# Buffer of the spectrum parts for a last transform: token pair outermost instead of channel half

## The chip, the cores and the metric

One core of a Trainium2 chip. The time is the device time of one execution in microseconds (us), as a median over several executions. A profile is one further execution, recorded by the hardware; its span runs from the first to the last instruction and is about 2 us shorter than the time. Of the engines, TensorE multiplies matrices, VectorE adds, ScalarE copies and applies functions, and the sync engine (SP) starts transfers (DMA); ScalarE starts some too. A trace also records the clock that TensorE was granted, 1.00 being full speed; it is called "half clock" at 0.50.

## The reference

Two branches on the same normalised input, added up, 2048 tokens of 512 channels:

```python
xn = _layernorm(x, axis=-1)
return x + _A_ref(xn, ...) + _B_ref(xn, ...)
# _A_ref: long convolution over the tokens by FFT of length 4096, plus u * Dskip
#   Yf = rfft(u, padded) * rfft(K, padded);  y = irfft(Yf)[:L]
# _B_ref: gated MLP of width 1792
#   h = sigmoid(x @ w_gate) * (x @ w_up);  return h @ w_down
```

The convolution is done as a transform in several stages of matmuls. What matters here is its last stage: it multiplies the "spectrum parts" by a constant matrix, and its result is added to that of the MLP.

## The kernel before: the parts that matter

The spectrum parts come from DRAM scratch (`v_scr`, one for each channel half p) into one SBUF buffer, 16 loads of 256 KB. Index p is the channel half (256 channels), t the token pair, r the token of the pair, j a half of the contraction.

```python
vall = at(0, [NP, 8, 2, 2, DW])        # NP = 2, DW = 256: [p, t, j, r, channel], 32 KB per partition
vps = [[vall[:, p, t] for t in range(8)] for p in range(NP)]
for t in range(8):
    for p in range(NP):
        ...   # dma("SP" if p == 0 or t % 2 == 0 else "ACT", vps[p][t], ...)   256 KB

def s2_mm(t, r, o, start, ps=(0, 1)):  # the last transform of one token pair
    kw = dict(stop=True, skip_group_check=True)
    i = 2 * t + r
    w = slice(DW * ps[0], DW * ps[-1] + DW)
    for j in range(2):
        T.matmul(o[:, w], s2[:, j, :], vall[:, ps[0]:ps[-1] + 1, t, j, r, :], start=start and j == 0, **kw)
    if i >= 12:
        T.matmul(o[:, w], sr[:, i - 12, :], rr[:, w], start=False, **kw)
```

One matmul thus reads 256 elements of each half. The program runs a fixed order of work (a long list in the source). Which instruction waits for which is not written by hand: the compiler layer derives it from the pieces of the buffers that each instruction reads and writes. Towards the end TensorE's order is: down projection of 14 matmuls; t=5; down projection; first row of t=6; t=0; second row of t=6; t=3; t=1; down projection; first row of t=7; t=4; t=2; down projection; the two channel halves of the last row of t=7. Line L994 is the `T.matmul` over `vall`, L996 the correction with `sr`, L1074 the down projection, L1009 and L1091 VectorE's additions, L973 the copy into `rr`, L417 every DMA issue.

## Time and profile before

| | before |
|---|---|
| time, median of the first three runs | 249.63 us (249.52 to 250.48) |
| span of the profiled run | 247.2 us |
| TensorE busy | 227.4 us, 92% |
| VectorE, ScalarE busy | 187.6 us, 181.6 us |
| idle of TensorE ahead of the last transform | 1.60 + 0.25 + 5.39 us |

A share of 92% suggests that little is to be had. Read by slices, TensorE is full until 217 us and has holes after that. The lines that show it are in the prediction. One more stretch matters later, the 3.4 us just ahead of the fall of the clock (length, busy time and count by engine, granted clock, DMA share, GB/s):

```profile
223.20:226.60 3.40, 1.37 (x7) 0.40 (x5) 1.82 (x2) 0.00 (x0) 0.00 (x0) 1.00 0.44 123
226.60:233.44 6.84, 3.48 (x9) 1.34 (x10) 0.98 (x2) 0.00 (x0) 0.00 (x0) 0.50 0.30 94
```

TensorE was busy for 1.37 of the 3.40 us, and then had half clock for 6.84 us.

### The profile page before, as it was taken

To read this page: it belongs to the slowest core of one execution; us is meant where nothing else is said; L and a number is where in the kernel's file an instruction comes from. 1 tells how busy PE (TensorE), PEld (TensorE's weight loads), DVE (VectorE), ACT (ScalarE), POOL (GpSimd) and SP (SyncE) were. 2 spreads that over 40 slices of the span, in tenths; PEclk is the share of its full clock that TensorE was granted. 3 is DMA by queue.
4 is the path that set the end of the run, shared out by engine and by line. 5 is a ranking of instruction groups with operands and counts; after the bars stand their busy time and mean duration, and the time that the engine had idled before them with its cause. 6 is when DMAs were issued, how large, how long until landed. Compare 5 with 4: busy or idle time off the path is not lost.

```text
span 247.2 us, 5353 instructions
## 1 busy us (share of the span) xinstructions
PE 227.4 (92%) x2045; PEld 114.2 (46%) x2074; DVE 187.6 (76%) x397; ACT 181.6 (73%) x294; POOL 18.4 (7%) x42
## 2 busy tenths in 40 slices
PE   7979999999999999999999999989999998972793
PEld 3545444444344643656556454366543553421341
DVE  3999899999999999999999999922344175512342
ACT  5989999999999986799988999764577785000000
POOL 1205200020000101000103100000000300000000
PEclk9999999999999999999999999999999999998699
DMA  6999775203496873756684676747776977935033
GB/s 153 213 376 334 246 264 127 87 11 74 137 231 216 164 191 97 165 172 191 140 223 109 208 199 163 174 133 231 198 195 217 187 228 196 266 89 180 16 140 115
DMA packets 50859, 43.60 MB, mean 176 GB/s; under 512 B 12561, under 2 KB 44050, under 8 KB 50834
## 3 DMA queue, kind: packets, MB, share of 16 engines
q1 hardware_dynamic: 48738, 40.58, 58.1%
q0 software_dynamic: 864, 1.57, 4.1%
q10 hardware_dynamic: 1232, 1.11, 1.5%
q8 instruction: 16, 0.26, 0.5%
q14 instruction: 9, 0.07, 0.1%
HBM read 24.64 MB, written 12.06 MB: 148 GB/s over the span
## 4 chain that ended last, share of the span: by engine, by line
PE 45%; ACT 21%; DMA 17%; SPq 7%; issue 5%; DVE 4%; ACTq 0%; DVEq 0%
PE bank L1074 12%; PE bank L1026 9%; DMA big<-v_scr 6%; PE bank L1041 5%; SPq L417 5%; PE pair L913 5%; PE pair L820 4%; ACT hT_sb L1035 4%; DMA big<-z_scr 4%; ACT big L697 3%; ACT big L666 3%; DMA wd_sb<-in_B_w_down_dram 3%; DMA wg_sb<-in_B_w_gate_dram 3%; PE pair L994 3%; ACT big L672 2%
## 5 line engine op out<-in xcount | busy, mean ns | idle before, releaser
L1026 PE MATMUL bank<-xnT,wg_sb 128*128 128x512 bf16 (+1 forms) x224 | 54.4, 368 | 2.6 <-DMA wg_sb<-in_B_w_gate_dram 1.0
L1041 PE MATMUL bank<-xnT,wu_sb 128*128 128x512 bf16 x215 | 53.5, 379 | 0.8 <-issue 0.3
L1074 PE MATMUL bank<-wd_sb,hT_sb 128*128 128x512 bf16 x217 | 50.5, 379 | 0.9 <-ACT glu_sb L1104 0.3
L1035 ACT ACTIVATE hT_sb<-bank 128x512 bf16<-128x512 f32 x56 | 33.2, 612 | 4.4 <-PE bank L1026 4.3
L1026 PEld LDWEIGHTS <-wg_sb 128*128 128x128 bf16 x236 | 21.6, 98 | 26.7 <-issue 5.3
L1074 PEld LDWEIGHTS <-hT_sb 128*128 128x128 bf16 x224 | 21.4, 98 | 26.2 <-issue 1.6
L1041 PEld LDWEIGHTS <-wu_sb 128*128 128x128 bf16 x224 | 21.2, 98 | 25.3 <-issue 2.0
L1056 DVE TENSOR_TENSOR hT_sb<-hT_sb,bank 128x512 bf16<-128x512 bf16 x36 | 23.9, 682 | 9.6 <-PE bank L1041 6.2
L919 DVE TENSOR_TENSOR big<-big 128x2048 bf16<-128x2048 bf16 x16 | 19.4, 1217 | 15.4 <-ACT big L915 8.0
L731 DVE TENSOR_TENSOR big<-big 128x1024 bf16<-128x1024 bf16 (+4 forms) x40 | 25.8, 644 | 0.6 <-ACT big L772 0.3
L732 DVE TENSOR_TENSOR big<-big 128x1024 bf16<-128x1024 bf16 (+4 forms) x40 | 25.7, 643 | 0.0
L913 PE MATMUL pair<-big 128*128 128x256 bf16 x160 | 19.8, 272 | 0.4 <-DVE big L855 0.3
L900 ACT ACTIVATE big<-pair 128x1024 bf16<-128x1024 f32 x16 | 16.3, 1025 | 4.3 <-PE pair L895 4.1
L915 ACT ACTIVATE big<-pair 128x1024 bf16<-128x1024 f32 x16 | 16.5, 1035 | 3.8 <-PE pair L913 3.1
L940 ACT ACTIVATE big<-pair 128x1024 bf16<-128x1024 f32 x16 | 16.3, 1033 | 2.8 <-PE pair L936 1.2
L913 PEld LDWEIGHTS <-big 128*128 128x128 bf16 x160 | 15.6, 98 | 5.5 <-issue 1.2
L697 ACT ACTIVATE big<-pair 128x1024 bf16<-128x1024 f32 x16 | 16.9, 1056 | 0.2 <-DMA z_scr<-big 0.2
L736 DVE TENSOR_TENSOR big<-big 128x512 bf16<-128x512 bf16 (+4 forms) x40 | 16.8, 420 | 0.2
L737 DVE TENSOR_TENSOR big<-big 128x512 bf16<-128x512 bf16 (+4 forms) x40 | 16.8, 419 | 0.0
L788 ACT ACTIVATE sq_sb<-big 128x256 bf16<-128x256 bf16 (+2 forms) x20 | 13.0, 655 | 2.6 <-DVE big L737 2.0
L666 ACT ACTIVATE big<-big 128x512 bf16<-128x512 f32 x24 | 14.0, 644 | 0.0
L772 ACT ACTIVATE big<-big 128x256 bf16<-128x256 bf16 x32 | 13.1, 454 | 1.1 <-PE pair L820 1.1
(106 smaller groups left out, 276.1 us busy)
## 6 DMA issues: line engine op xcount, KB each, us to landing
big<-c_E SPq DMA_DIRECT2D x16, 320.0 KB, 4.2
z_scr<-big SPq DMA_DIRECT2D x16, 256.0 KB, 2.6
big<-z_scr SPq DMA_DIRECT2D x16, 256.0 KB, 4.3
big<-big SPq DMA_DIRECT2D x64, 64.0 KB, 3.1
v_scr<-big SPq DMA_DIRECT2D x16, 256.0 KB, 3.0
big<-v_scr SPq DMA_DIRECT2D x12, 256.0 KB, 4.6
big<-in_A_u_dram SPq DMA_DIRECT2D x4, 512.0 KB, 5.5
wu_sb<-in_B_w_up_dram SPq DMA_DIRECT2D x2, 896.0 KB, 8.7
```

What stands on the lines that cost most here:

```text
L666: S.activation(out=W[p][:, k], in_=cur[:, :, DW * p:DW * p + DW], func=ACT.Identity)
L697: ev = pl.add("ACT", 0.90, lambda sl=sl, zs=zs: S.activation(out=zs().rearrange("p j d -> p (j d)"), in_=two(sl), func=ACT.Identity), [fx_ ...
L731: V.tensor_tensor(out=wide(outp), in0=wide(lo), in1=mre, op=ALU.mult)
L732: V.tensor_tensor(out=wide(tb()), in0=wide(lo), in1=mim, op=ALU.mult)
L736: V.tensor_tensor(out=outp[:, :, :, 0, :], in0=outp[:, :, :, 0, :], in1=tb()[:, :, :, 1, :], op=opr)
L913: T.matmul(two(sk)[:, o:o + DW], es()[:, g, kt, :], kT[p][:, kt, :], start=kt in (0, NKT - 1), stop=kt >= NKT - 2)
L919: V.tensor_tensor(out=pp().rearrange("p q h m -> p (q h) m"), in0=xx().rearrange("p q h m -> p (q h) m"), in1=kb()[:, 0:2 * DW].unsqueeze( ...
L1026: T.matmul(bank(sl)[:, c0:c1], w[:, kt, k * 128:(k + 1) * 128], xnT[:, grp, kt, c0:c1], start=(kt == 0), stop=(kt == KT - 1))
L1035: S.activation(out=hT_sb[:, hs.idx, k % 2, :], in_=bank(sl), func=ACT.Sigmoid)
L1041: T.matmul(bank(sl), wu_sb[:, kt, k * 128:(k + 1) * 128], xnT[:, grp, kt, :], start=(kt == 0), stop=(kt == KT - 1))
L1056: V.tensor_tensor(out=h(), in0=h(), in1=us_sb[:, us.idx, :] if on else bank(sl), op=ALU.mult)
L1074: T.matmul(bank(po), hT_sb[:, hts[k // 2].idx, k % 2, jj * 128:(jj + 1) * 128], wd_sb[:, k, :], start=(k == 0), stop=k == FT - 1, **kw)
```

## The change

Its intent is that all that belongs to one token pair lies together, so that a read of one pair spans no other pair's parts.

```diff
-    vall = at(0, [NP, 8, 2, 2, DW])
-    vps = [[vall[:, p, t] for t in range(8)] for p in range(NP)]
+    vall = at(0, [8, NP, 2, 2, DW])
+    vps = [[vall[:, t, p] for t in range(8)] for p in range(NP)]
@@ s2_mm
-            T.matmul(o[:, w], s2[:, j, :], vall[:, ps[0]:ps[-1] + 1, t, j, r, :], ...)
+            T.matmul(o[:, w], s2[:, j, :], vall[:, t, ps[0]:ps[-1] + 1, j, r, :], ...)
```

More of the change, by code (lines that the diff above doesn't have):

```diff
@@ L993, in s2_mm @@
         for j in range(2):
-            T.matmul(o[:, w], s2[:, j, :], vall[:, ps[0]:ps[-1] + 1, t, j, r, :], start=start and j == 0, **kw)
+            T.matmul(o[:, w], s2[:, j, :], vall[:, t, ps[0]:ps[-1] + 1, j, r, :], start=start and j == 0, **kw)
         if i >= 12:
```

## The prediction

> **What bounds the kernel now.** I read the page's slices first, then the chain that ended last, then the last 40 us engine by engine, because the change touches one buffer that is only read at the end. The slices:
>
> ```profile
> PE   7979999999999999999999999989999998972793
> ...
> PEclk9999999999999999999999999999999999998699
> ```
>
> Up to slice 35 TensorE is the bound, busy nine tenths or more at full clock. From slice 36 (222 us) that breaks: 7, 2, 7, and the granted clock falls in the same place. So 25 us at the end are limited by something else. The chain over 208 us to the end (start, length, what) says what:
>
> ```profile
> 211.22 7.31 DMA big<-v_scr
> 218.53 0.05 issue
> 218.58 1.05 PE pair L994 x4
> 219.63 0.02 issue
> 219.65 3.19 DMA big<-v_scr
> 222.84 0.05 issue
> 222.89 0.61 PE bank L994 x2
> ...
> 225.92 0.34 SPq L417
> 226.26 0.05 issue
> 226.32 3.61 DMA big<-v_scr
> 229.92 0.04 issue
> 229.96 1.01 PE bank L994 x2
> 230.98 0.43 PE bank L996
> 231.40 2.79 PE pair L994 x8
> ```
>
> Three times the last transform (L994) waits for a load of spectrum parts into `vall`, until 218.58, 222.89 and 229.96. TensorE's timeline gives the idle times as 1.60, 0.25 and 5.39 us. Why are those loads so late? ScalarE's queue and the waits of the sync engine's queue answer:
>
> ```profile
> 210.59 9.58 ACTq L417 DMA_DIRECT2D big<-v_scr  x3
> 220.22 0.59 ACT L973 ACTIVATE big<-pair 8x512 bf16<-8x512 f32 x1 [9.51 <-PE pair L994]
> ...
> SPq L417 <- PE bank L994: 10.5, 1, 10.5
> ```
>
> Queue instructions that only start loads of `v_scr` wait for matmuls of L994 on ScalarE (9.5 us, the rr copy stuck behind) and on the sync engine (10.5 us, once). A load into a slot that no matmul has read yet should wait for no matmul.
>
> The cost of the long wait is more than its length (busy time and count by engine, granted clock, DMA share, GB/s):
>
> ```profile
> 224.60:229.96 5.36, 0.00 (x0) 0.10 (x1) 1.82 (x2) 0.00 (x0) 0.00 (x0) 0.69 0.65 196
> 229.96:233.40 3.44, 3.44 (x9) 1.20 (x9) 0.94 (x2) 0.00 (x0) 0.00 (x0) 0.50 0.00 0
> ```
>
> After the hole the matmuls run at half clock until about 233.4.
>
> **What the compiled program says.** I listed the semaphore waits of the kernel before as compiled (a list of instructions, no time in it). Write p for the channel half and t for the token pair. A matmul of pair t reads `vall[:, 0:2, t, j, r, :]`: 256 elements of p=0 and 256 of p=1. With p outermost these lie 16 KB apart, and the dependence tracker treats everything between as read. So the first one (t=5) waits not only for its own parts (0,5) and (1,5), but for (0,6), (1,0), (1,1), every other load ahead of it in program order that lies in that interval. The other way round, load (1,3) waits for the matmuls of t=5, and load (1,4) for those of t=6 (as if it overwrote them), and the matmuls of the second row of t=6 wait for (1,4) and (1,2). None of these is a true dependence.
>
> **What the Trainium skill says.** "Perfetto Trace Analysis", section "Identifying Dependency Chains", says to look at the instruction's own text for the semaphores it waits on, and that extra conditions can sit in an event instruction ahead of it; that is how I found the list above, and the trace has such event instructions on L994. "TensorE: Matmul & The Clock Gate", section "What's actually happening", gives half clock after an idle window of about 3.4 us and full clock after a busy one. The trace agrees: the mean of 0.69 over 224.60 to 229.96 means that 62% of it, 3.3 us, was at 0.50, so the half clock began at 226.6 and lasted to about 233.4, two such windows. "DMA: Bandwidth & Descriptors", section "Queues, rings and completion order", says each DMA engine takes turns between the queues' rings and takes a ring in order; so a load that is added behind another on the same queue should not slow that one much. The trace of before cannot show that. No page bears on how waits are derived from access patterns.
>
> **The change part by part.** It removes and adds no instruction: the same 16 loads of 256 KB, the same matmuls, the same order on each queue. Each load still writes 2 KB in a row per partition, each matmul still moves 2 x 256 elements. What changes is the address: the four reads of pair t now lie inside a block of 4 KB that belongs to t alone. All false waits go, in both directions. The half (0,t) moves up to at most 28 KB; the tables that lived there are last read by L820, whose last group ends at 163.8, and the first load of `vall` is issued at 165.18, so no new wait comes in.
>
> Now the tail again, in TensorE's unchanged order, with full-clock durations from the same trace. The first matmul needs (1,5), whose semaphore in the trace is complete at 217.00, not (1,1), complete at 218.53. The down projection before it ends at 216.98 (218.58 less 1.60). So:
> - t=5: 217.05 + 1.05 = 218.10.
> - Down projection of 14 matmuls, 3.02 (as 239.59 to 242.61): 221.12.
> - t=6 first row with its correction matmul, 0.65 (as 237.22 to 237.87): 221.77.
> - t=0, 0.88 (as 223.71 to 224.59): 222.65. t=6 second row: 223.30.
> - t=3 and t=1, 1.73 (as 237.87 to 239.60): 225.03.
> - Down projection: 228.05. t=7 first row: 228.70. t=4 and t=2: 230.43. Down projection: 233.45.
>
> In the kernel before the last of these ends at 242.62. Difference 9.17 us, which is: 1.53 (first wait), 0.24 and 0.17 (second wait, and the slow start after it), 5.37 (third wait), 0.79 and 1.07 (matmuls of t=6, t=3, t=1 at half clock). What follows, the last two half rows, two additions and the stores, is 4.58 us in both. All of the 9.17 lies on the path that sets the end.
>
> Is everything else there in time? Loads: (1,3) is issued about 212.7, just behind (1,1); (1,4) about 213.5, when its semaphore lane is free (212.97); (1,7) after the rr copy, about 215. All loads before them had landed at 218.5. At the 320 to 380 GB/s that the DMA view shows from 213 to 216 these three, 768 KB, take some 2.4 us more: by 221. (1,3) is needed at 223.3, (1,7) at 228.05, (1,4) at 228.7. Load (1,2) keeps its place behind the store of t=0, which waits for VectorE: t=0 ready at 222.65, addition 1.23 us, store issued 224.0, load issued 224.4, landed 3.6 later, 228.0; needed by t=2 at 229.6. VectorE: additions of t=0, t=6 (two of 0.68), t=3 end about 226.5, t=1 about 227.8 (it waits for a store to free its buffer); TensorE needs their PSUM at 228.7 and 229.6. It fits, with 1 to 3 us of slack each.
>
> **Rivals.**
> 1. The waits are real or come from somewhere else, so nothing moves: 249.6. For it: the three waits are all named as DMA, and the profile names only the last releaser. Against: the queue waits on L994 for 10.5 us, and the list of waits.
> 2. The loads are hidden no better, because the traffic is the limit. The DMA share is 0.92 from 209 to 217. If loads issued earlier slow (1,5), the first wait comes back: at worst 1.5 us, time 242. If load (1,2) behind the stores turns out late, t=2 waits 1 or 2 us, and the last down projection with it: 242 too. A short hole like that would not halve the clock.
> 3. The hole at 224.6 goes but the clock stays low, say by a hole of over 2 us elsewhere: 1.9 us of the gain lost, 242.3.
> 4. A layout cost: operand halves 2 KB apart instead of 16 KB. L994 matmuls at full clock have the same 379 ns as L1074's with contiguous operands, so I see no penalty to gain or lose: 0.
>
> **Range and chances.** 249.63 - 9.2 = 240.4 us. Rivals 2 and 3 push up by at most about 2; downwards I see 1 us (first matmuls after no wait start faster, 0.88 for 1.05; fewer event instructions; stores earlier). Range 239.3 to 242.3. Faster by over 2% means below 244.6; only rival 1 or two of the others together get there: 0.96, 0.03, 0.01.
>
> **What would show it.** Span near 238. In the chain no load of `v_scr` after the first t=5; no wait of the queues on L994; the idle time of L994 below 0.5 us in all but the last half row (0.51 for VectorE, which stays); granted clock 1.00 from 217 on; rr copy at 214 in place of 220; everything before 209 unchanged. It would be wrong if the sync queue still waits for L994, if (1,5) lands after 218, or if the chain shows stores or VectorE between the groups of L994.

## The result

240.56 us median (240.04 to 241.47, 4 runs) against 249.81 us of the kernel before (4 runs). The ratio is 0.963, 95% interval 0.959 to 0.967. Ratios here are the mean time of one kernel's fast runs over that of the other's of the same rounds, so not quite the ratio of the medians quoted. The instructions on each engine are the same ones in the same order. The slices of the changed kernel (PE is the busy share of TensorE in tenths, PEclk its granted clock in tenths):

```profile
PE   7989999999999999999999999999999989799993
...
PEclk9999999999999999999999999999999999999999
```

The dips at the end and the fall of the clock are gone. The chain that ended last, from 211 us to 228 us:

```profile
211.74 5.70 DMA big<-v_scr
217.44 0.02 issue
217.46 1.02 PE pair L994 x4
218.48 3.02 PE bank L1074 x14
221.50 0.43 PE bank L994 x2
221.93 0.21 PE bank L996
222.15 0.86 PE pair L994 x4
223.01 0.43 PE bank L994 x2
223.44 0.22 PE bank L996
223.66 1.75 PE pair L994 x8
225.41 3.02 PE bank L1074 x14
```

After t=5 no load stands in the chain, to its end: one TensorE group follows on the other, and the last two half rows alternate with VectorE's additions. (The chain dates the load from 211.74, the issue of (1,1). By the semaphores the last one that t=5 waits for is (1,5), issued at 211.10 and complete at 217.41; (1,1) was complete at 219.19, after t=5 had started.) The queues, in the same two places as before, ScalarE's timeline and then the sync queue's waits (engine and line, waited for: total, times, longest):

```profile
211.10 2.27 ACTq L417 DMA_DIRECT2D big<-v_scr  x3
214.41 0.59 ACT L973 ACTIVATE big<-pair 8x512 bf16<-8x512 f32 x1 [3.23 <-PE pair L971]
...
SPq L417 <- DVE big L1009: 13.9, 6, 4.5
SPq L417 <- ACT big L940: 3.8, 2, 2.4
SPq L417 <- DMA big<-in_A_u_dram: 2.2, 1, 2.2
```

ScalarE's three loads go out in 2.27 us instead of 9.58, and the copy into `rr` runs at 214.4 instead of 220.2. The sync queue's wait of 10.5 us for L994 is gone; what it waits for now (L1009) are stores that wait for VectorE's results.

### The profile page after: what moved, and what is told of

Same layout as the page of the kernel before. It is cut to its first block, busy times and chain, and to the rows that moved or that the text cites. A ratio compares the mean times of both kernels' runs of the same rounds, so it can differ in the third digit from the quotient of the medians.

```text
span 238.5 us, 5382 instructions
## 1 busy us (share of the span) xinstructions
PE 227.5 (95%) x2074; PEld 113.8 (48%) x2074; DVE 187.5 (79%) x397; ACT 181.6 (76%) x294; POOL 18.4 (8%) x42
## 4 chain that ended last, share of the span: by engine, by line
PE 42%; ACT 24%; DMA 14%; DVE 7%; SPq 6%; issue 5%; ACTq 0%; DVEq 0%
PE bank L1074 15%; DMA big<-big 9%; PE bank L1026 7%; ACT hT_sb L1035 5%; SPq L417 4%; PE pair L913 4%; PE bank L1041 4%; ACT big L666 3%; PE pair L820 3%; ACT big L697 3%; DMA wg_sb<-in_B_w_gate_dram 3%; ACT big L672 3%; DVE big L919 2%; DMA big<-v_scr 2%; ACT big L558 2%
## 5 line engine op out<-in xcount | busy, mean ns | idle before, releaser
L1026 PE MATMUL bank<-xnT,wg_sb 128*128 128x512 bf16 (+1 forms) x236 | 55.4, 369 | 1.6 <-DMA wg_sb<-in_B_w_gate_dram 0.9
L1041 PE MATMUL bank<-xnT,wu_sb 128*128 128x512 bf16 x224 | 54.5, 380 | 0.1
L919 DVE TENSOR_TENSOR big<-big 128x2048 bf16<-128x2048 bf16 x16 | 19.4, 1219 | 16.1 <-DMA big<-big 6.8
L936 PE MATMUL pair<-big 64*64 64x512 bf16 (+1 forms) x256 | 13.0, 327 | 1.4 <-DVE big L919 1.4
```

The lines of the kernel that those rows point to most:

```text
L919: V.tensor_tensor(out=pp().rearrange("p q h m -> p (q h) m"), in0=xx().rearrange("p q h m -> p (q h) m"), in1=kb()[:, 0:2 * DW].unsqueeze( ...
L1026: T.matmul(bank(sl)[:, c0:c1], w[:, kt, k * 128:(k + 1) * 128], xnT[:, grp, kt, c0:c1], start=(kt == 0), stop=(kt == KT - 1))
L1041: T.matmul(bank(sl), wu_sb[:, kt, k * 128:(k + 1) * 128], xnT[:, grp, kt, :], start=(kt == 0), stop=(kt == KT - 1))
```

## The experiments

Two theories stood against each other. The first: the gain is that of waits that were never needed, since a strided read counts as a read of all that lies between its pieces. The second: the addresses themselves matter, where the loads write or how far apart the two pieces lie. Each experiment but the last two starts from the kernel before. Line numbers shift by a few in some; L996, L997, L998 and L999 are then the `vall` matmul or its correction.

**1. Layout of before, reads split.**

```diff
+        for qs in [(q,) for q in ps]:
+            w = slice(DW * qs[0], DW * qs[-1] + DW)
             for j in range(2):
-                T.matmul(..., vall[:, ps[0]:ps[-1] + 1, t, j, r, :], ...)
+                T.matmul(..., vall[:, qs[0]:qs[-1] + 1, t, j, r, :], ...)
```

> The layout of before (halves 16 KB apart), but each matmul of the last transform reads one half only, so no read spans another pair's parts; twice as many matmuls, half as wide. Theory (false waits from the span of a read): no load waits for a matmul, no hole before the last half row, clock 1.00 to the end, time as after: 240.5, at most 0.5 more for the extra weight loads. Rival (the addresses themselves matter, where the loads write or how far apart the operand's halves lie): the loads go where they went before, so most of the hole stays, 247 to 250.

Measured: 240.64 us, ratio 0.963 (0.960 to 0.966), the same as the change. TensorE's timeline:

```profile
217.32 1.20 PE L997 MATMUL pair<-big 128*128 128x256 bf16 x8
218.36 3.18 PE L1077 MATMUL bank<-wd_sb,hT_sb 128*128 128x512 bf16 x14
221.38 0.38 PE L997 MATMUL bank<-big 128*128 128x256 bf16 x2
```

No idle time stands in brackets. Every load writes where it wrote before, and the whole gain is there. That rules out the addresses of the loads.

**2 and 3. Halves 4 KB apart, two groupings.** Pairs share a block by twos; in the second kernel which two is chosen so that each false wait is for a load that lands early.

```diff
-    vall = at(0, [NP, 8, 2, 2, DW])
-    vps = [[vall[:, p, t] for t in range(8)] for p in range(NP)]
+    vall = at(0, [NP * 8, 2, 2, DW])
+    place = {t: n for n, t in enumerate(range(8))}                   # experiment 2
+    place = {t: n for n, t in enumerate((0, 1, 4, 2, 3, 7, 5, 6))}   # experiment 3
+    unit = lambda p, t: place[t] // 2 * 4 + place[t] % 2 + 2 * p
+    vps = [[vall[:, unit(p, t)] for t in range(8)] for p in range(NP)]
@@ s2_mm
-            ... vall[:, ps[0]:ps[-1] + 1, t, j, r, :] ...
+            ... vall[:, unit(ps[0], t):unit(ps[-1], t) + 1:2, j, r, :] ...
```

> Halves 4 KB apart, so that pairs 0 and 1, 2 and 3, 4 and 5, 6 and 7 share a block and have false waits only within it. Theory: the first and the second wait are gone, but the matmuls of t=3 now wait for load (1,2), which sits on the sync queue behind the store of t=0: one hole of about 4.5 us before t=3, from 223.6 to 228.1, with or without a time at half clock after it: 245 to 246.5. Rival (distance matters): close to after, 240.5 to 241.5.

> Halves 4 KB apart as in the run before, but blocks shared by pairs 0 and 1, 4 and 2, 3 and 7, 5 and 6: there are still false waits, each on a load that has landed long before. Theory: a false wait costs only if its releaser is late, so as after: 240.5 within 0.7, no hole. Rival (distance, or any false wait costs): same as the run with the natural grouping.

Measured: 248.24 us (ratio 0.993, 0.988 to 0.997) for the natural grouping, 240.66 us (0.965, 0.959 to 0.971) for the other. The regrouped kernel has no idle time ahead of t=3 and t=1:

```profile
225.85 1.91 PE L996 MATMUL pair<-big 128*128 128x512 bf16 x8
```

The same distance gives nearly nothing or the whole gain, by grouping alone. So distance is not the cause, and neither is the bare number of foreign parts that a read spans (one in both kernels). What counts is whether the load falsely waited for comes late. In the first of the two kernels that load is (1,2), which has its place on the sync queue behind the store of t=0. Its chain:

```profile
222.79 1.24 DVE big L1011
224.03 0.02 issue
224.05 0.34 SPq L417
224.39 0.05 issue
224.44 3.43 DMA big<-v_scr
227.87 0.05 issue
227.92 3.60 PE pair L996 x8
```

The addition of t=0, its store, the load, then t=3: a loop through VectorE and two DMA issues that t=3 does not need. The hole came as expected, until 227.9. The time did not: 1.7 us over the range. The windows say why:

```profile
224.00:229.00 5.00, 1.08 (x3) 0.44 (x4) 1.22 (x3) 0.00 (x0) 0.00 (x0) 0.79 0.36 105
229.00:232.00 3.00, 3.00 (x8) 1.06 (x7) 1.67 (x2) 0.00 (x0) 0.00 (x0) 0.50 0.02 7
232.00:236.00 4.00, 3.95 (x15) 1.62 (x15) 0.78 (x1) 0.00 (x0) 0.00 (x0) 0.78 0.52 192
```

By the trace the clock was at half from 226.92 to 233.74, and matmuls ran in 5.8 us of that. The eight matmuls of t=3 and t=1 took 3.60 us instead of 1.73, the down projection after them 4.18 instead of 3.02: 3 us of loss. In the kernel before the matmuls came late in the half-clock stretch and lost less. So a shorter hole (4.57 us) cost more after it than a longer one.

**4 and 5. Fill the hole.** Idle matmuls into an unused bank of PSUM (the memory that takes TensorE's results), in the kernel before (23, ahead of the second row of t=6) and in experiment 2 (19, ahead of t=3).

```diff
         i = 2 * t + r
+        if i == 13:                      # i == 6 and 19 in the other
+            for _ in range(23):
+                T.matmul(banks[2][:], hT_sb[:, 0, 0, 0:128], wd_sb[:, 0, :], start=True, stop=True)
```

> The kernel before with 23 idle matmuls of 512 columns (their result is not used) put on TensorE just ahead of the second row of t=6, where the hole of 5.4 us is. The false waits stay. Theory: the hole is filled and stays as long, but the clock no longer halves: the terms for half clock, 0.79 and 1.07 us, are saved, 247.8 to 248.2, granted clock 1.00 from 224 on. Rival: the half clock is not caused by the hole (a fixed time after the start, or the power drawn): unchanged 249.8 with 0.50 in the same place.

> The run with halves 4 KB apart came out at 248.2 instead of 245 to 246.5; its profile has the hole that was expected (4.57 us before t=3) but 3 us of half clock cost rather than at most 1: the half clock lasted 6.8 us, nearly all of it over matmuls. Here 19 idle matmuls fill that hole. If that reading is right: hole and false wait stay, clock 1.00 to the end, 248.2 - 3.0 = 245.2, within 0.7. If something else held it up: 247 or more.

Measured: 247.53 us (ratio 0.992, 0.989 to 0.995), by medians 1.84 us less than before, where the prediction's two terms for half clock add up to 1.86. And 244.81 us (ratio 0.981, 0.977 to 0.986) for the filled one of experiment 2. That is 3.4 us less than without by medians, 2.8 by the ratios (the two did not run in the same rounds); 3.0 was expected. Useless work made both kernels faster, since it kept the clock up. The window of the hole, filled, in the kernel before:

```profile
224.60:229.96 5.36, 4.88 (x24) 2.22 (x23) 1.76 (x2) 0.00 (x0) 0.00 (x0) 1.00 0.65 196
229.96:233.40 3.44, 3.44 (x18) 1.55 (x17) 2.71 (x3) 0.00 (x0) 0.00 (x0) 1.00 0.00 0
```

The granted clock is 1.00 in both stretches, and in the second 18 matmuls fit where the kernel before had 9.

**6. Only t=5 split.** The edit of experiment 1, for t == 5 alone.

> The kernel before with the reads of the first pair used, t=5, split into halves, the others left as they were. Theory, term by term: the first wait (1.53) and the second (0.24 and 0.17) go, the hole before the second row of t=6 stays, since load (1,4) still waits for the first row of t=6 and load (1,2) sits behind the stores; then the clock halves. The terms of the working give 249.4 - 1.9 = 247.5; [...]247 to 248.5. A hole of about 5.3 us that ends near 228. Rival (the three waits overlap, so the first two are absorbed by the third): 249.4.

Measured: 248.04 us (ratio 0.994, 0.989 to 0.998).

```profile
217.40 0.81 PE L997 MATMUL pair<-big 128*128 128x256 bf16 x6 [0.22 <-DMA big<-v_scr]
...
221.07 0.59 PE L997 MATMUL bank<-big 128*128 128x512 bf16 x2
...
228.25 1.01 PE L997 MATMUL bank<-big 128*128 128x512 bf16 x2 [5.51 <-DMA big<-v_scr]
```

The first wait is down to 0.22 us, the second is gone, and the hole ends 1.7 us earlier than before. It is as long as before: what comes earlier ahead of it moves it whole. Of the 1.7 about 1.1 went to the clock: half clock lasted from 227.10 to 233.93, and the work from the hole's end through the next down projection took 8.35 us instead of 7.26.

**7. Only t=6 split**, the pair that the profile names at the long wait.

> The kernel before with only the reads of t=6 split, the pair in front of which TensorE stood idle for 5.4 us. Theory: the hole only moves on by one group, since the matmuls of t=3 span load (1,2) as well: about 4.7 us of idle before t=3, ending near 229.5, then half clock. The first wait of 1.5 stays. 248 to 249.5, a gain of 1.4 at most. Rival (what the profile names, a wait of t=6, is the cause by itself): the 5.4 us and the half clock go, 242 to 243.

Measured: 248.91 us over its three fast runs (ratio 0.997, 0.991 to 1.002; the fourth run, 252.0 us, was slow). No gain can be told. The chain:

```profile
226.05 0.34 SPq L417
226.40 0.05 issue
226.45 3.59 DMA big<-v_scr
230.04 0.04 issue
230.08 3.60 PE pair L997 x8
```

The second row of t=6 no longer waits, and t=3, next in line, waits for the same load until 230.08. The waiter that a profile names is the first in line, not all of the cause.

**8. Loads first, layout of before.** The four loads that follow the first matmul in program order are moved ahead of it.

```diff
+        early = (623, 625, 631, 621)          # loads (1,3), (1,4), (1,7), (1,2)
+        seq = [n for n in ORDER if n not in early]
+        at_ = seq.index(619) + 1              # behind load (1,1)
+        seq[at_:at_] = early
-        for n in ORDER or range(len(self.ops)):
+        for n in seq:
```

> The kernel before with the four late loads moved ahead of the first matmul of the last transform in program order, layout as before. No load can wait for a matmul any more (that direction is gone), but the first matmul, t=5, spans all loads from (0,5) to (1,5), now among them (1,2), (1,3), (1,4). Theory: one hole of 4 to 4.5 us in front of t=5, until about 221.5, then none; 244.5 without a time at half clock, up to 247.5 with one, as in the run with 4 KB. Rival (only loads that wait for matmuls cost): 240.5 to 241.

Measured: 246.71 us (ratio 0.989, 0.985 to 0.994).

```profile
222.15 1.87 PE L998 MATMUL pair<-big 128*128 128x512 bf16 x4 [4.54 <-DMA big<-v_scr]
223.81 3.91 PE L1078 MATMUL bank<-wd_sb,hT_sb 128*128 128x512 bf16 x14
...
217.00:221.60 4.60, 0.61 (x3) 0.19 (x2) 0.00 (x0) 0.00 (x0) 0.00 (x0) 1.00 0.84 275
221.60:225.00 3.40, 2.85 (x7) 0.99 (x7) 0.95 (x1) 0.00 (x0) 0.00 (x0) 0.54 0.02 5
```

With one direction of false waits gone (loads for matmuls), the other (the first matmul for all loads in its span) makes a hole of 4.54 us, and half clock follows. Both directions count. Reordering alone does not replace the layout.

**9. Can more be had? The last row in two halves**, on the changed kernel, beside that kernel again.

```diff
-    for k in range(FT):                       # last down projection, 512 columns in one bank
-        T.matmul(bank(po), hT..., wd_sb[:, k, :], ...)
+    # 256 columns into one PSUM bank, last transform of that half; then 256 into another bank
+    down(0); s2_mm(7, 1, bank(po), False, (0,))
+    down(256)                                 # VectorE adds and SP stores the first half meanwhile
```

> The changed kernel, with the last down projection done in two halves of 256 columns, each in a PSUM bank of its own, and the first half finished (last transform, addition, store) while the second is being multiplied. In the changed kernel the second half row waits 0.52 us for VectorE's addition to the first, since both lie in one bank. 28 matmuls at about 0.109 us each take 3.05 us instead of 3.02. The second half row then ends at once: about 0.6 us less than the changed kernel beside it, so about 239.9 against 240.5. If the last addition isn't on the path, or weight loads are not hidden with 256 columns: no gain or a loss of up to 1 us.

> The changed kernel again, beside the run with the last halves on the same chip: 240.5, ratio to before 0.963 as measured first. Only for that comparison.

Measured in five rounds: 239.86 us (ratio to before 0.961, 0.958 to 0.965) and 240.15 us (0.963, 0.959 to 0.966) for the changed kernel beside it. In the profile the idea works: TensorE's last groups are

```profile
230.57 1.69 PE L1074 MATMUL bank<-wd_sb,hT_sb 128*128 128x256 bf16 x14
232.09 0.38 PE L994 MATMUL bank<-big 128*128 128x256 bf16 x2
232.31 0.27 PE L996 MATMUL bank<-big 128*128 128x256 bf16 x1
232.42 1.69 PE L1074 MATMUL bank<-wd_sb,hT_sb 128*128 128x256 bf16 x14
233.95 0.38 PE L994 MATMUL bank<-big 128*128 128x256 bf16 x2
```

with no idle time between the halves, where the changed kernel waits 0.52 us. But the two intervals overlap nearly whole. A gain of 0.3 us is possible and not shown.

## Why the prediction was right

- *False waits as the cause.* Shown from two sides: experiment 1 removes them without the layout, experiment 3 keeps the strided reads and false waits but makes them harmless, and both come out with the change. Rival 1 (nothing moves) has fallen. Rival 3 did not come true in the profiled run: the granted clock is 1.00 until 237.50, after the last matmul. Rival 4 has fallen too: `vall` matmuls at full clock have a median of 379 ns before and after.
- *The sum.* Predicted from the first matmul of t=5 to the end of the last down projection: 217.05 to 233.45, 16.40 us. Measured: 217.46 to 233.82, 16.36 us. Counted from the start of t=5, the groups hit their place to 0.1 us. The span was 238.5 instead of 238.0 mainly because t=5 came 0.4 us later, and so had the last projection ahead of it (214.24 against 213.78), in a stage that the change does not touch: there TensorE waited 1.43 instead of 0.73 us for VectorE (L919, until 206.4). The other 0.1 us lies behind the last projection. So "everything before 209 unchanged" held only to half a microsecond. Other profiles shift too: t=5 starts at 217.15 in that of experiment 2 and at 219.81 in that of experiment 3, after the half clock at 199 us named below; that run (242.83 us) is the slowest of its four.
- *The first wait, 1.53.* The term holds as a cause: the first matmul no longer waits for (1,1). In experiment 6 it shrank to 0.22. It ends where predicted, at the landing of (1,5), which by now lands as the down projection ends.
- *Half clock, 0.79 + 1.07.* Experiment 4 confirms the term and its size roughly. That 1.84 by medians meets the 1.86 so closely is luck: the interval of its ratio means 1.3 to 2.9 us. In its trace the groups from the end of the hole to the next down projection take 2.53 instead of 4.24 us, so 1.71, and the hole ended 0.28 us earlier besides. It is a term of this kernel, not a constant: in experiment 2 the same kind of stretch cost 3 us. The expectations of experiment 2 took over the small size, and there missed by 1.7 us.
- *What the prediction had wrong about the clock.* It says that the trace agrees with half clock after an idle window of about 3.4 us. The half clock did last two such times (6.83 us), but it began 2.0 us after the last matmul had ended (224.57, 226.61), so the 3.4 us before it were not idle. Under rivals 2 and 3 it says that a hole of 1 or 2 us would not halve the clock and one of over 2 us might. In the profiled run of experiment 3 a wait of 2.10 us for a load (until 198.55) was followed by half clock from 199.37 to 202.78, so that limit has hardly any room. Nothing of the 9.17 us rests on either sentence; the upper end of the range did.
- *Rival 2, the traffic.* Three more loads were issued while (1,5) was in flight. It took 6.3 us from issue to completion (211.10 to 217.41), before 6.4 (210.59 to 217.00). Two of the three went behind it on its own queue, ScalarE's. The Trainium skill, "DMA: Bandwidth & Descriptors", section "Queues, rings and completion order", says a ring is taken in order, from which the prediction concluded that what is queued behind should not delay it much; this trace agrees. The third went on the sync engine's queue, behind two loads that were there before as well. Load (1,2) was issued at 224.75 (predicted 224.4) and nothing waited for it.
- *The terms cannot be removed one at a time.* The sum counted 5.37 us for the long wait. Experiment 7 removed its named waiter and gained nothing that can be told. The prediction used the terms only for the change as a whole, where they do add up.

## What to carry to other kernels

Where a framework derives waits from access patterns, lay a shared buffer out so that what one instruction reads in a stride is one block that nothing else writes; splitting the read does the same. Look in the profile for a load that waits for a matmul which never used its slot, and list the waits of all later readers before you believe that removing the named one helps. Count a hole on TensorE with the half clock that may follow it: here it cost some 1.8 us more after a hole of 5.4 us and 3.0 us more after one of 4.6, and nothing after the first wait of 1.6 us.

## What the Trainium skill lacked or had wrong

- No page has it: how waits come out of strided access patterns, and that the interval between the pieces counts. "Perfetto Trace Analysis", section "Identifying Dependency Chains", sends the reader to the waits of an instruction but not to this cause. Worth here: 249.4 against 240.6 us with the loads' addresses unchanged.
- "TensorE: Matmul & The Clock Gate", section "What's actually happening", has the clock fall after an idle window of about 3.4 us. In the kernel before it fell at the end of a window (223.2 to 226.6) in which TensorE was busy for 1.37 us of 3.40. Laid over the other traces, windows of 3.41 us that end where the clock changed (or a whole number of windows away) give: it also fell after one that was 38% busy (195.96 to 199.37, experiment 3) and one that was 39% busy (240.57 to 243.98, experiment 2), and did not after one of 44% (232.95 to 236.36, experiment 9) and one of 47% (242.20 to 245.62, experiment 7). So here a window need not be idle: up to 40% busy the clock fell.
- Same section: back at full clock after a busy window. How busy is not said. A window from 226.92 with matmuls from 227.92 on (about 70%) did not lift it in experiment 2, and half clock lasted 6.83 us; one from 221.84 with matmuls from 222.15 on (about 90%) did in experiment 8, after 3.41 us. In between nothing was measured.
